# Attention for one query position: two K loads joined, and the last head's output split over two engines

## The chip, the cores and the metric

The kernel runs on one core of a Trainium2 chip. Times are device microseconds of one execution. Before the change, three runs gave 320.42, 319.57 and 319.09 us: a median of 319.57 us.

## The reference

```
q: (1, 16, 1, 256)   k, v: (1, 16, 8192, 256)   all bf16
scores = einsum("bhqd,bhkd->bhqk", q, k) * 256 ** -0.5
p      = softmax(scores)
out    = einsum("bhqk,bhkd->bhqd", p, v)      # (1, 16, 1, 256), bf16
```

There is one query row for each of 16 heads. Each head reads 8192 keys and 8192 values of 256 numbers once: 4.19 MB of K and 4.19 MB of V, so 134 MB in all.

## The kernel before

A head's K lies in a buffer of 128 partitions by 64 columns, where a column is one key's 256 numbers; partition p holds keys 64p to 64p + 63. There are two K buffers (`kbuf`, halves for even and odd heads) and two V buffers (`vbuf`). The DMA queue of SP carries every load in one written order (`ORDER`): `k0 k1 v0 k2 v1 k3 v2 ... k6 k7 v5 k8 ... k14 v12 k15 v13 v14 v15`. Most loads are whole heads (4096 KB). `CUTS` lists those that are cut into pieces at given columns, each piece a load of its own: k0 and k15 at column 34, and v13, v14 and v15. Every piece has a semaphore. For k0 and k15 the first piece shares the semaphore of all even or odd K loads (`k0`, `k1`), and the second has one named `kb`.

SP issues a load when its buffer is free. A K load of head h waits until VectorE (`kd`) and GpSimd (`tp`) have done with head h - 2 (L119, L120). A V load of head h waits for `pr`, which TensorE raises after the weighted sum of head h - 2 (L122).

The work of one head:

- Scores, columns 0 to 23: GpSimd multiplies four columns at once by the query (L182), and ScalarE sums each product along the row (L382). Two products may be under way (`sp`).
- Scores, columns 24 to 63: VectorE multiplies and sums one column in one instruction (L208), in four chunks of ten (loop over `c`). After the first chunk of head h it also takes the reciprocal of the softmax sum of head h - 2 (L195, `recips`) and the maximum of head h - 1 over the partitions (L199, `xmax`).
- The maximum: VectorE takes each partition's (L225), TensorE transposes that (L316), VectorE reduces it (L199), and TensorE spreads it to all partitions (L302).
- ScalarE takes the exponentials (L347, `expo`), in the middle of the next head's products.
- TensorE multiplies the exponentials by V (L265, `doubles`), two columns to a matmul, sums the exponentials (`total`, L252), and after ScalarE's drain of the sums (L358, `collect`, behind the last product of a head) gathers them into `ob` (L278). `ob` holds a head's 256 outputs as two halves, one in row 0 and one in row 32.
- ScalarE divides by the sum and writes row 0 and row 32 of `o_all` (L364, `final`), three heads behind.

TensorE goes through 18 rounds, one head's weighted sum two rounds after its scores. Each round waits for that round's maximum (`g`), then does the weighted sum, the total and the gather, and then waits for the next maximum (`m`).

Head 15 ends differently. The first 28 columns of its V go as above. The other 36 are multiplied straight into `ob` (L323), with a wait for each later piece of v15 (48 and 60). Then VectorE, and not ScalarE, divides (L231) rows 0 and 32 with those in between in one instruction. SP stores heads 0 to 14 (waiting for v15's last piece), then head 15 as two half rows of 256 B, and waits for both.

In the loop of VectorE the waits before each chunk are `k_waits` (the query's copy, and both K semaphores) and then, for the second piece of a cut load,

```
dve.wait_ge(sem("kb"), (h * 8 + c + 119) // 120 * 16 + 16)
```

which asks for k0's second piece from chunk 1 of head 0 on, and for k15's from chunk 1 of head 15 on. GpSimd has no such wait, since its columns all lie in the first piece.

Of the kernel before, what the change touches and what calls it, by code (L numbers as in the profile page):

```python
# [11 lines left out]
NPL = 24  # L12
GRP = 4
CH = 10
CUTS = {"k0": (0, 34), "k15": (0, 34), "v13": (0, 48), "v14": (0, 40), "v15": (0, 28, 48, 60)}
ORDER = "k0 k1 v0 k2 v1 k3 v2 k4 v3 k5 v4 k6 k7 v5 k8 v6 k9 v7 k10 v8 k11 v9 k12 v10 k13 v11 k14 v12 k15 v13 v14 v15"
LAST_PAIRED = 28
STRIP = 64
BLK = 32
ROWS = 97  # L20
AHEAD = {"k1": 16, "kb": 16, "sp": 2, "pr": 1, "cm": 2, "pv": 1, "fin": 3, "rc": 3, "ex": 1, "mT": 1, "g": 1, "nb": 1}
STREAM_AHEAD = ("v0", "v1", "v0_40", "v1_48")


def bass_standalone__mha_softmax__decode_kernel(nc: bass.Bass, q: bass.AP, k: bass.AP, v: bass.AP, out: bass.AP):
# [19 lines left out]
    def load(kind, h):  # L45
        cuts = CUTS.get(f"{kind}{h}", (0,)) + (J,)
        for n, (a, b) in enumerate(zip(cuts, cuts[1:])):
            name = "kb" if kind == "k" and n else f"{kind}{h % 2}" + (f"_{a}" if n else "")
            stream.append((kind, h, a, b, name))

    for name in ORDER.split():
# [2 lines left out]
    with contextlib.ExitStack() as ctx:  # L54

        def sb(name, shape, d):
            return ctx.enter_context(nc.sbuf_tensor(name, shape, d))
# [34 lines left out]
        identb = sb("identb", [P, P], BF16)  # L92
        ones_row = sb("ones_row", [1, P], FP32)
        ones_col = sb("ones_col", [P, 1], FP32)
        o_all = sb("o_all", [BLK + 1, H * HW], out.dtype)

        acc = ps("acc", [P, 2 * D])
        ob = ps("ob", [P, 512])
# [15 lines left out]
        @(lambda f: f(nc.sync))  # L114
        def _(sp):
            for kind, h, a, b, name in stream:
                if h >= 2 and a == 0:
                    if kind == "k":
                        sp.wait_ge(sem("kd"), (h - 1) * NC)  # L119
                        sp.wait_ge(sem("tp"), (h - 1) * NG)  # L120
                    else:
                        sp.wait_ge(sem("pr"), h + 2)  # L122
                buf = kbuf[:, h % 2 * J * D :] if kind == "k" else vbuf[h % 2]
                sp.dma_start(buf[:, a * D : b * D], src(k if kind == "k" else v, h)[:, a * D : b * D]).then_inc(  # L124
                    sem(name), 16
                )
            two = out.rearrange("b h s (two d) -> two (b h s) d", two=2)
            for a, b in ((0, LAST), (LAST, H)):
                if b < H:
                    sp.wait_ge(sem(stream[-1][-1]), 16)  # L130
                sp.wait_ge(sem("fin"), b + 3)
                rows = o_all[0 : BLK + 1 : BLK, a * HW : b * HW].rearrange("two (h d) -> two h d", d=HW)
                sp.dma_start(two[:, a:b, :], rows).then_inc(sem("o"), 16)
            sp.wait_ge(sem("o"), 32)
            sp.nop()

# [54 lines left out]
        @(lambda f: f(nc.vector))  # L191
        def _(dve):
            def recips(h, n, after=0):
                dve.wait_ge(sem("pr"), h - n + (3 + after))
                dve.reciprocal(recip[:, ds(back(h, n), 1)], tot[0 : BLK + 1, :]).then_inc(sem("rc"), 1)  # L195

            def xmax(h, n):
                dve.wait_ge(sem("mT"), h - n + 2)
                dve.tensor_reduce(g[:, :], mx[0:1, 0:P], AX.X, ALU.max).then_inc(sem("g"), 1)  # L199

            with dve.Fori(0, H) as h:
                par = dve.snap(h % 2)
                with dve.Fori(0, NC) as c:  # L203
                    k_waits(dve, h)
                    dve.wait_ge(sem("kb"), (h * 8 + c + 119) // 120 * 16 + 16)  # L205
                    for b in range(CH):
                        col = kbuf[:, ds(par * (J * D) + c * (CH * D) + (NPL + b) * D, D)]
                        ins = dve.scalar_tensor_tensor(  # L208
                            out=col,
                            in0=col,  # L210
                            scalar=SCALE,
                            in1=qrow[:, ds(par * 512, D)],
                            op0=ALU.mult,
                            op1=ALU.mult,
                            accum_out=S[:, ds(h * J + c * CH + (NPL + b), 1)],
                        )
                    ins.then_inc(sem("kd"), 1)
                    with dve.If(c == 0):
                        with dve.If(h > 1):
                            recips(h, 2)  # L220
                        with dve.If(h > 0):
                            xmax(h, 1)
                dve.wait_ge(sem("kd"), h * NC + NC)  # L223
                dve.wait_ge(sem("sp"), h * NG + (NG + 2))
                dve.tensor_reduce(m[:, :], S[:, ds(h * J, J)], AX.X, ALU.max).then_inc(sem("m"), 1)  # L225
            recips(LAST, 1)
            xmax(LAST, 0)
            recips(LAST, 0, 1)
            dve.wait_ge(sem("rc"), H + 3)
            dve.wait_ge(sem("pv"), H + 4)  # L230
            dve.tensor_scalar(  # L231
                out=o_all[:, LAST * HW : H * HW],
                in0=ob[0 : BLK + 1, 0:HW],
                scalar1=recip[:, LAST:H],
                scalar2=None,
                op0=ALU.mult,
            ).then_inc(sem("fin"), 1)
# [95 lines left out]
        @(lambda f: f(nc.scalar))  # L333
        def _(act):
            def q_copy(h):
                act.wait_ge(sem("qp"), h + 1)
                par = 0 if isinstance(h, int) else act.snap(h % 2)
                act.activation(out=q_now[:, ds(par * D, D)], in_=qrow[:, ds(par * 512, D)], func=ACT.Copy).then_inc(  # L338
                    sem("qb"), 1
                )  # L340

            def expo(h, n):
                act.wait_ge(sem("bc"), h - n + 2)
                act.activation(out=negb[:, :], in_=sm, func=ACT.Copy, scale=-1.0).then_inc(sem("nb"), 1)  # L344
                act.wait_ge(sem("nb"), h - n + 2)
                i = back(h, n)
                act.activation(  # L347
                    out=E[:, ds(i % 2 * EW, J)].rearrange("p (two x) -> p x two", two=2),
                    in_=S[:, ds(i * J, J)].rearrange("p (x two) -> p x two", two=2),
                    func=ACT.Exp,  # L350
                    bias=negb[:, :],
                    scale=1.0,
                    accum_out=lsum[:, :],
                ).then_inc(sem("ex"), 1)

            def collect(h, n):
                act.wait_ge(sem("pr"), h - n + 4)
                act.activation(out=comb[:, :], in_=acc[0:ROWS, :], func=ACT.Copy).then_inc(sem("cm"), 1)  # L358

            def final(h, n):  # L360
                act.wait_ge(sem("rc"), h - n + 4)
                act.wait_ge(sem("pv"), h - n + 4)
                i = back(h, n)
                act.activation(  # L364
                    out=o_all[:, ds(i * HW, HW)],
                    in_=ob[0 : BLK + 1, 0:HW],
                    func=ACT.Copy,
                    scale=recip[:, ds(i, 1)],
                ).then_inc(sem("fin"), 1)

            act.dma_start(q_sb[:, :], q[0, :, 0, :]).then_inc(sem("ldq"), 16)
            act.preload_act_table(ACT.Exp)
            q_copy(0)
            with act.Fori(0, H + 2) as h:
                with act.If(h < H):
                    q_copy(h + 1)
                with act.Fori(0, NG) as i:
                    with act.If(h < H):
                        act.wait_ge(sem("tp"), h * NG + i + 1)
                        for b in range(GRP):  # L380
                            part = prod[:, ds(i % 2 * (GRP * D) + b * D, D)]
                            ins = act.activation(  # L382
                                out=part,
                                in_=part,
                                func=ACT.Copy,
                                scale=SCALE,
                                accum_out=S[:, ds(back(h, 0) * J + i * GRP + b, 1)],
                            )
                        ins.then_inc(sem("sp"), 1)
                    with act.If(i == 1):  # L390
                        with act.If(h > 0):
                            with act.If(h < H + 1):
                                expo(h, 1)
                        with act.If(h > 2):
                            final(h, 3)
                with act.If(h > 1):
                    collect(h, 2)
            act.nop()


# [26 lines left out]
```

## Time and profile before

| | before |
|---|---|
| median of three runs | 319.57 us |
| the profiled execution | 318.72 us |
| its span in the profile | 317.1 us |
| granted TensorE clock, mean | 0.726 |
| VectorE busy | 232.5 us (73%) |
| GpSimd busy | 204.3 us (64%) |
| ScalarE busy | 190.6 us (60%) |
| TensorE matmuls busy | 123.5 us (39%) |
| read from memory | 134.23 MB, 423 GB/s over the span |
| load queue's packets | 98.7% of the 16 DMA engines' span |

In the profile PE is TensorE, DVE is VectorE, ACT is ScalarE, POOL is GpSimd and SP is SyncE; a q behind the name (DVEq, SPq) is that engine's instruction queue, where waits, register work and the issue of transfers happen. L208 is line 208 of the kernel. A row of the timeline gives a start, a length, the engine and the line, output and input, and in square brackets how long the engine had stood idle and what ended that. A row of groups gives the count, the busy time and the mean in ns. A row of the chain of waits gives start, length and what it was spent on; a load's length there runs from its issue to its landing.

### The profile page before, as it was taken

To read this page: it belongs to the slowest core of one execution; us is meant where nothing else is said; L and a number is where in the kernel's file an instruction comes from. 1 tells how busy PE (TensorE), PEld (TensorE's weight loads), DVE (VectorE), ACT (ScalarE), POOL (GpSimd) and SP (SyncE) were. 2 spreads that over 40 slices of the span, in tenths; PEclk is the share of its full clock that TensorE was granted. 3 is DMA by queue.
4 is the path that set the end of the run, shared out by engine and by line. 5 is a ranking of instruction groups with operands and counts; after the bars stand their busy time and mean duration, and the time that the engine had idled before them with its cause. 6 is when DMAs were issued, how large, how long until landed. Compare 5 with 4: busy or idle time off the path is not lost.

```text
span 317.1 us, 7815 instructions
## 1 busy us (share of the span) xinstructions
PE 123.5 (39%) x832; PEld 60.9 (19%) x832; DVE 232.5 (73%) x1329; ACT 190.6 (60%) x865; POOL 204.3 (64%) x115
## 2 busy tenths in 40 slices
PE   3001116262372723527182521706227061361855
PEld 1000003031130301213030310302113030121423
DVE  0797979497694967969797969679395893969700
ACT  2476737477373864777666757647386473868510
POOL 3788758395683857869686848578384874886400
PEclk9999999657565685757665585765957567585799
DMA  7999999999999999999999999999999999999995
GB/s 303 429 459 409 451 434 426 442 418 451 409 463 397 463 397 463 401 459 401 459 417 442 426 434 442 417 455 405 463 397 463 397 463 401 436 434 409 434 424 243
DMA packets 5685, 134.25 MB, mean 423 GB/s; under 512 B 676, under 2 KB 692, under 8 KB 948
## 3 DMA queue, kind: packets, MB, share of 16 engines
q1 hardware_dynamic: 5652, 134.23, 98.7%
q10 hardware_dynamic: 32, 0.01, 0.0%
q8 instruction: 1, 0.02, 0.0%
HBM read 134.23 MB, written 0.01 MB: 423 GB/s over the span
## 4 chain that ended last, share of the span: by engine, by line
DMA 56%; DVE 21%; issue 10%; DVEq 9%; PE 2%; SPq 1%
DMA kbuf<-in_k_dram 42%; DVE kbuf L208 20%; DMA vbuf<-in_v_dram 14%; DVEq L208 6%; PE acc L265 2%; DVEq L205 1%; DVEq L203 1%; DVEq L140 1%; SPq L124 1%; DVEq L139 0%; PE ob L323 0%; DVE g L199 0%; DVE recip L195 0%; DVEq L223 0%; DVEq L195 0%
## 5 line engine op out<-in xcount | busy, mean ns | idle before, releaser
L208 DVE SCALAR_TENSOR_TENSOR kbuf<-kbuf,qrow x640 | 223.8, 417 | 53.8 <-issue 27.8
L182 POOL TENSOR_TENSOR prod<-kbuf,q_now 128x1024 f32 x96 | 201.8, 2123 | 89.8 <-DMA kbuf<-in_k_dram 60.8
L382 ACT ACTIVATE prod<-prod x384 | 154.5, 403 | 74.9 <-POOL prod L182 68.6
L265 PE MATMUL acc<-vbuf,E 128*64 128x512 bf16 x494 | 85.5, 521 | 31.8 <-DMA vbuf<-in_v_dram 31.2
L382 ACT ACTIVATION_READ_ACCUMULATOR prod<-prod x384 | 71.7, 187 | 0.0
L208 DVE DVE_READ_ACCUMULATOR kbuf<-kbuf,qrow x640 | 52.8, 83 | 0.0
L265 PEld LDWEIGHTS acc<-vbuf,E 128*64 128x64 bf16 x494 | 36.2, 148 | 74.7 <-issue 34.4
L302 PE MATMUL mx<-g,ones_row 1*128 1x1 f32 x34 | 9.7, 351 | 75.5 <-DVE g L199 75.5
L278 PE MATMUL ob<-comb,sel 97*1 97x128 f32 x144 | 14.4, 335 | 52.0 <-ACT comb L358 52.0
L338 ACT ACTIVATE q_now<-qrow (+1 forms) x17 | 6.5, 383 | 28.7 <-PE qrow L242 28.6
L302 PEld LDWEIGHTS mx<-g,ones_row 1*128 1x128 f32 x34 | 8.2, 298 | 79.9 <-DVE g L199 79.5
L316 PE MATMUL mx<-ident,m 128*1 128x128 f32 x32 | 8.3, 352 | 25.9 <-DVE m L225 25.9
L278 PEld LDWEIGHTS ob<-comb,sel 97*1 97x1 f32 x144 | 5.6, 91 | 55.0 <-ACT comb L358 53.3
L225 DVE TENSOR_REDUCE m<-S 128x1 f32 x16 | 3.5, 220 | 13.8 <-ACT prod L382 12.5
L358 ACT ACTIVATE comb<-acc 97x512 f32<-97x512 f32 x16 | 9.2, 576 | 6.7 <-PE tot L252 6.7
L347 ACT ACTIVATE E<-S,negb x16 | 9.3, 583 | 4.1 <-ACT negb L344 4.1
L195 DVE RECIPROCAL recip<-tot 33x1 f32 (+1 forms) x16 | 2.5, 155 | 10.6 <-PE tot L252 10.6
L316 PEld LDWEIGHTS mx<-ident,m 128*1 128x1 f32 x32 | 3.1, 103 | 28.3 <-DVE m L225 26.9
L242 PE MATMUL qrow<-q_sb,identb 16*128 16x256 bf16 x18 | 6.0, 347 | 4.6 <-DMA q_sb<-in_q_dram 4.6
L364 ACT ACTIVATE o_all<-ob,recip 33x128 f32 x15 | 5.4, 362 | 1.4 <-PE ob L278 1.4
L347 ACT ACTIVATION_READ_ACCUMULATOR E<-S,negb 128x1 f32 x16 | 5.3, 330 | 0.0
L344 ACT ACTIVATE negb<-mx 128x1 f32<-128x1 f32 x16 | 2.5, 157 | 4.0 <-PE mx L302 4.0
(26 smaller groups left out, 23.3 us busy)
## 6 DMA issues: line engine op xcount, KB each, us to landing
kbuf<-in_k_dram SPq DMA_DIRECT2D x14, 4096.0 KB, 21.1
vbuf<-in_v_dram SPq DMA_DIRECT2D x13, 4096.0 KB, 27.1
kbuf<-in_k_dram SPq DMA_DIRECT2D x2, 2176.0 KB, 13.3
kbuf<-in_k_dram SPq DMA_DIRECT2D x2, 1920.0 KB, 17.5
vbuf<-in_v_dram SPq DMA_DIRECT2D x1, 3072.0 KB, 29.9
vbuf<-in_v_dram SPq DMA_DIRECT2D x1, 2560.0 KB, 19.7
vbuf<-in_v_dram SPq DMA_DIRECT2D x1, 1792.0 KB, 10.6
vbuf<-in_v_dram SPq DMA_DIRECT2D x1, 1536.0 KB, 23.0
```

What stands on the lines that cost most here:

```text
L182: pool.tensor_tensor(out=prod[:, b * GRP * D : (b + 1) * GRP * D].rearrange("p (b d) -> p b d", b=GRP), in0=kbuf[:, ds(par * (J * D) + i * ...
L208: ins = dve.scalar_tensor_tensor(out=col, in0=col, scalar=SCALE, in1=qrow[:, ds(par * 512, D)], op0=ALU.mult, op1=ALU.mult, accum_out=S[:, ...
L242: pe.matmul(qrow[:, ds(at * 512, D)], lhsT=identb[0:H, col].to_broadcast([H, P]), rhs=q_sb[:, :], start=True, stop=True,).then_inc(sem("qp ...
L265: ins = pe.matmul(acc[at : at + STRIP, :], lhsT=E[:, par * EW + j // 2 :][:, 0:STRIP], rhs=vbuf[par][:, j * D : (j + 2) * D], start=(j < 4 ...
L278: ins = pe.matmul(ob[row : row + 1, 0:HW], lhsT=sel[:, n : n + 1], rhs=comb[:, n * D + a : n * D + a + HW], start=(n == 0), stop=(n == 1), ...
L302: pe.matmul(sm, lhsT=ones_row[:, :], rhs=g[:, :], start=True, stop=True).then_inc(sem("bc"), 1)
L316: pe.matmul(mx[0:1, 0:P], lhsT=m[:, :], rhs=ident[:, :], start=True, stop=True).then_inc(sem("mT"), 1)
L338: act.activation(out=q_now[:, ds(par * D, D)], in_=qrow[:, ds(par * 512, D)], func=ACT.Copy).then_inc(sem("qb"), 1)
L347: act.activation(out=E[:, ds(i % 2 * EW, J)].rearrange("p (two x) -> p x two", two=2), in_=S[:, ds(i * J, J)].rearrange("p (x two) -> p x ...
L358: act.activation(out=comb[:, :], in_=acc[0:ROWS, :], func=ACT.Copy).then_inc(sem("cm"), 1)
L364: act.activation(out=o_all[:, ds(i * HW, HW)], in_=ob[0 : BLK + 1, 0:HW], func=ACT.Copy, scale=recip[:, ds(i, 1)],).then_inc(sem("fin"), 1)
L382: ins = act.activation(out=part, in_=part, func=ACT.Copy, scale=SCALE, accum_out=S[:, ds(back(h, 0) * J + i * GRP + b, 1)],)
```

## The change

- k0 and k15 leave `CUTS`: each is one load of 4096 KB with one semaphore. VectorE's wait on `kb` goes from its loop, and the semaphore with it.
- The last head's output: ScalarE, after its loop, divides row 0 of `ob` into the first 128 numbers of a new one-row tile `o_last`, and VectorE divides row 32 into the other 128. `o_all` keeps heads 0 to 14. The last store waits for both and writes `o_last`, one row of 512 B.
- Where a wait for the sums in `ob` (`pv`) stood behind the wait for the reciprocal (`rc`), it now stands ahead of it: in VectorE's last operation and in ScalarE's `final`.

```
-CUTS = {"k0": (0, 34), "k15": (0, 34), "v13": (0, 48), "v14": (0, 40), "v15": (0, 28, 48, 60)}
+CUTS = {"v13": (0, 48), "v14": (0, 40), "v15": (0, 28, 48, 60)}
...
-            name = "kb" if kind == "k" and n else f"{kind}{h % 2}" + (f"_{a}" if n else "")
+            name = f"{kind}{h % 2}" + (f"_{a}" if n else "")
...
-        o_all = sb("o_all", [BLK + 1, H * HW], out.dtype)
+        o_all = sb("o_all", [BLK + 1, LAST * HW], out.dtype)
+        o_last = sb("o_last", [1, D], out.dtype)
...
-            two = out.rearrange("b h s (two d) -> two (b h s) d", two=2)
-            for a, b in ((0, LAST), (LAST, H)):
-                if b < H:
-                    sp.wait_ge(sem(stream[-1][-1]), 16)
-                sp.wait_ge(sem("fin"), b + 3)
-                rows = o_all[0 : BLK + 1 : BLK, a * HW : b * HW].rearrange("two (h d) -> two h d", d=HW)
-                sp.dma_start(two[:, a:b, :], rows).then_inc(sem("o"), 16)
+            sp.wait_ge(sem(stream[-1][-1]), 16)
+            sp.wait_ge(sem("fin"), LAST + 3)
+            sp.dma_start(
+                out.rearrange("b h s (two d) -> two (b h s) d", two=2)[:, 0:LAST, :],
+                o_all[0 : BLK + 1 : BLK, :].rearrange("two (h d) -> two h d", d=HW),
+            ).then_inc(sem("o"), 16)
+            sp.wait_ge(sem("fin"), H + 4)
+            sp.dma_start(out[0, LAST, :, :], o_last[:, :]).then_inc(sem("o"), 16)
...
-                    dve.wait_ge(sem("kb"), (h * 8 + c + 119) // 120 * 16 + 16)
...
+            dve.wait_ge(sem("pv"), H + 4)
             dve.wait_ge(sem("rc"), H + 3)
-            dve.wait_ge(sem("pv"), H + 4)
+            row, a = halves[1]
             dve.tensor_scalar(
-                out=o_all[:, LAST * HW : H * HW],
-                in0=ob[0 : BLK + 1, 0:HW],
-                scalar1=recip[:, LAST:H],
+                out=o_last[:, a : a + HW],
+                in0=ob[row : row + 1, 0:HW],
+                scalar1=recip[0:1, LAST:H],
...
             def final(h, n):
+                act.wait_ge(sem("pv"), h - n + 4)
                 act.wait_ge(sem("rc"), h - n + 4)
-                act.wait_ge(sem("pv"), h - n + 4)
...
+            act.wait_ge(sem("pv"), H + 4)
+            act.wait_ge(sem("rc"), H + 3)
+            act.activation(out=o_last[:, 0:HW], in_=ob[0:1, 0:HW], func=ACT.Copy, scale=recip[0:1, LAST:H]).then_inc(
+                sem("fin"), 1
+            )
```

More of the change, by code (lines that the diff above doesn't have):

```diff
@@ L20 @@
 ROWS = 97
-AHEAD = {"k1": 16, "kb": 16, "sp": 2, "pr": 1, "cm": 2, "pv": 1, "fin": 3, "rc": 3, "ex": 1, "mT": 1, "g": 1, "nb": 1}
+AHEAD = {"k1": 16, "sp": 2, "pr": 1, "cm": 2, "pv": 1, "fin": 3, "rc": 3, "ex": 1, "mT": 1, "g": 1, "nb": 1}
 STREAM_AHEAD = ("v0", "v1", "v0_40", "v1_48")
```

## The prediction

> **What bounds the kernel now.** I read the page first for the share of each engine and of the DMA, then stretches of the span for the DMA's rate, then the chain of work that ended last, then the waits near both ends, where the change acts.
>
> From the page, the DMA row of the 40 slices and the queue that carries the loads:
>
> ```profile
> DMA  7999999999999999999999999999999999999995
> ...
> q1 hardware_dynamic: 5652, 134.23, 98.7%
> ```
>
> No compute engine is busy over 73% of the span, but the 16 DMA engines are at 9 tenths or more in every slice but the first and the last. The same in numbers, by stage: the middle, where only whole loads run; the stretch that holds the cut k15; the last stretch, with the cut V loads (columns: stretch, its length, five busy times, granted clock, DMA share, GB/s).
>
> ```profile
> core 0: us, PE busy (x) PEld busy (x) DVE busy (x) ACT busy (x) POOL busy (x), PEclk, DMA share, GB/s
> 42.20:246.20 204.00, 85.78 (x518) 41.60 (x517) 159.43 (x913) 129.77 (x594) 138.72 (x66) 0.66 1.00 432
> 246.20:292.40 46.20, 15.07 (x96) 7.69 (x96) 37.03 (x213) 30.02 (x139) 33.71 (x17) 0.65 1.00 428
> 292.40:314.00 21.60, 15.34 (x155) 7.95 (x157) 7.01 (x40) 7.37 (x30) 4.11 (x2) 0.89 1.00 421
> ```
>
> The share is 1.00 throughout, so the time is bytes over rate: 134.23 MB at 432 GB/s is 310.7 us of the span's 317.1. The bytes do not change. What the change can move is the start, the end, the few per cent between 421 and 432 GB/s, and any gap that it opens in the queue. A whole 4.19 MB load takes 4.19/0.432 = 9.7 us.
>
> The end of the chain of work that ended last (start, length, what):
>
> ```profile
> 299.20 14.74 DMA vbuf<-in_v_dram
> 313.94 0.04 issue
> 313.99 1.08 PE ob L323 x32
> 315.07 0.03 issue
> 315.09 0.02 DVEq L230
> 315.11 0.05 issue
> 315.17 0.34 DVE o_all L231
> ```
>
> The third piece of v15 lands at 313.94; from there it is 1.08 us of matmuls, 0.10 us until VectorE starts, 0.34 us of its one operation, and then the last store: 317.1 - 315.51 = 1.59 us.
>
> **Part 1: k0 in one piece.** Head 0's scores now wait for the whole of k0. Rows: VectorE's first column and the first of its second chunk, which waited for the second piece; from the chain, k0's and k2's loads; and the load of k8, for comparison.
>
> ```profile
> 9.50 0.42 DVE L208 SCALAR_TENSOR_TENSOR kbuf<-kbuf,qrow  x1 [9.50 <-issue]
> ...
> 13.68 0.42 DVE L208 SCALAR_TENSOR_TENSOR kbuf<-kbuf,qrow  x1 [0.68 <-DMA kbuf<-in_k_dram]
> ```
>
> ```profile
> 1.19 11.87 DMA kbuf<-in_k_dram
> ...
> 24.40 17.79 DMA kbuf<-in_k_dram
> ...
> 135.51 13.03 DMA kbuf<-in_k_dram
> ```
>
> The second piece landed at 1.19 + 11.87 = 13.06 and VectorE ran on 0.62 us later. With one piece the first chunk starts at about 13.7 in place of 9.50. VectorE had three chunks left at 13.68 and ended them at 24.40, 3.6 us each; now it has four, and ends at about 28.0. It is k2's load that waits for this (its buffer holds k0), so k2 is issued 3.6 us later. Cover: k2 was issued at 24.40 and landed at 42.19, so with 9.7 us of its own the load ahead of it, v0, ended at about 32.5. The issue stood 8.1 us ahead of that; it will stand 4.5 us ahead. Is that enough? k8 was issued at 135.51 and landed at 148.54, so only 3.3 us before its forerunner ended at about 138.8, and the engines stayed full there:
>
> ```profile
> 136.00:140.00 4.00, 1.76 (x11) 0.71 (x11) 1.76 (x10) 1.75 (x8) 3.14 (x2) 0.50 1.14 492
> ```
>
> (A share over 1 is a packet counted where it ended.) So I cost the delay at nothing. The next load that it could hurt is v2, which waits for head 0's weighted sum, which waits for the first chunk of head 2:
>
> ```profile
> 53.04 0.33 SPq L124 DMA_DIRECT2D vbuf<-in_v_dram  x1
> ```
>
> Its forerunner k3 ends at about 42.19 + 2 x 9.7 = 61.6, 8.6 us later; a delay of 3.6 us leaves 5.0. By head 3 it is gone, since a load pair takes 19.4 us and VectorE's head some 16.5 (below). If this cover failed, each microsecond past it would cost one.
>
> **Part 2: k15 in one piece.** GpSimd's head-15 rows, VectorE's first head-15 column and head 14's and 15's maximum, ScalarE's drain after head 15 (L358, issued behind its last product):
>
> ```profile
> 266.34 4.20 POOL L182 TENSOR_TENSOR prod<-kbuf,q_now 128x1024 f32 x2 [5.60 <-DMA kbuf<-in_k_dram]
> ...
> 281.12 4.20 POOL L182 TENSOR_TENSOR prod<-kbuf,q_now 128x1024 f32 x2 [0.82 <-DMA kbuf<-in_k_dram]
> ```
>
> ```profile
> 282.42 0.22 DVE L225 TENSOR_REDUCE m<-S 128x1 f32 x1 [1.22 <-ACT prod L382]
> 284.17 0.42 DVE L208 SCALAR_TENSOR_TENSOR kbuf<-kbuf,qrow  x1 [1.53 <-issue]
> ...
> 298.98 0.22 DVE L225 TENSOR_REDUCE m<-S 128x1 f32 x1 [0.26 <-DVE kbuf L208]
> ```
>
> ```profile
> 298.39 0.57 ACT L358 ACTIVATE comb<-acc 97x512 f32<-97x512 f32 x1
> ```
>
> GpSimd started head 15 at 281.12, as the first piece landed. The second, 30 of 64 columns or 1.97 MB, needs 4.6 us more at 428 GB/s: k15 is whole at 285.7. VectorE's head took 298.98 - 284.17 = 14.8 us, with its gap of 1.5 to 2 some 16.5; it starts at about 286.4 and ends near 301, so GpSimd with ScalarE decides. Head 14 shows that pair from a start set by the DMA: 266.34 to 282.42 is 16.1 us. So head 15's maximum comes at 285.7 + 16.1 = 301.8, 2.8 us later, and ScalarE's drain about 3.1 later. Bounds: GpSimd's whole 4.6, and the 2.2 by which VectorE's start moves. Take 3.1. Behind the drain stand TensorE's gather of head 13, the maximum's transpose, head 14's weighted sum, and head 15's. What TensorE waits for between 301 and the end:
>
> ```profile
> PE acc L265 <- DMA vbuf<-in_v_dram: 3.2, 3, 1.5
> PE ob L278 <- ACT comb L358: 1.5, 2, 0.8
> PE ob L323 <- DMA vbuf<-in_v_dram: 0.6, 1, 0.6
> ```
>
> In one chain it waits 3.2 + 0.6 = 3.8 us for loads that keep their times. A delay of 3.1 is eaten up there, with 0.7 to spare. Cost 0; at the upper bound 4.6 - 3.8 = +0.8 us.
>
> **Part 3: two cuts fewer.** SP issues two loads less (0.33 us each in the rows above, hidden by a queue that is full). Does a cut cost DMA time? The last stretch runs at 421 for 432 GB/s: 2.5% of 21.6 = 0.55 us over five extra pieces, 0.11 each. So two cuts give -0.2 us. Bounds: 0, and -2.1 if k0's whole start-up excess (13.06 less the 9.7 of a load, less 1.7 for the issue and the first bytes: the first slice's digit 7 leaves 1.6 to 2.4 of its 7.9 us idle) were the cut's, 1.7, and the 0.43 us (4/432 of 46.2) of the stretch with k15 too.
>
> **Part 4: the wait on "kb" leaves VectorE's loop.** Its register work:
>
> ```profile
> L205 DVEq FUSED_REGOPS  x64: 218/218/222, 8.6 to 294.4; - x64
> ```
>
> 64 x 0.218 = 14 us of VectorE's queue, much of it beside running columns. No load waits for VectorE with an empty queue, so it is worth 0 on the path (it trims the delays of parts 1 and 2 by up to 0.2 a chunk, which I leave out).
>
> **Part 5: the last head's output.** Before, one VectorE operation on 33 partitions; now ScalarE scales row 0 and VectorE row 32 into one row. ScalarE's last work before, its form of the operation, and both output stores:
>
> ```profile
> 310.88 0.60 ACT L358 ACTIVATE comb<-acc 97x512 f32<-97x512 f32 x1 [2.29 <-PE tot L252]
> ```
>
> ```profile
> L364 ACT ACTIVATE o_all<-ob,recip 33x128 f32 x15 | 5.4, 362 | 1.4 <-PE ob L278 1.4
> ```
>
> ```profile
> L133 SPq DMA_DIRECT2D out_dram<-o_all x2: 526/598/670, 314.6 to 315.5; - x2
> ```
>
> Columns per partition stay 128, so each operation keeps its time: 0.34 on VectorE, 0.36 on ScalarE, side by side: +0.02. The swapped order of the two waits: in the chain above the separate wait instruction is the later-written one, L230, and the operation starts 0.08 after it. With the reciprocal's wait written last, that one passes early: -0.05 to -0.08. ScalarE's last drain ends at 311.48, 3.6 us before the last matmul does, so its new instruction waits ready. Side by side or one after the other is shown by no row; if the two reads of one PSUM bank took turns, +0.36.
>
> [...]
>
> The last store carries 512 B as one row in place of two half rows. No row shows that shape: 0, with bounds of -0.2 (issue at the 0.33 of a wide load for 0.53) and +0.15 (the 0.67 of the longer store).
>
> **Sum.** 0 + 0 - 0.2 + 0 - 0.05 + 0 = -0.25 us on the profiled execution's 318.72, which itself stands 0.85 below the median of 319.57. On the median: 319.3.
>
> **Rivals.** (a) The end overruns: part 2's delay reaches TensorE at its full 4.6 us, in place of 3.1. For it: ScalarE stops for the exponentials in mid-head, so GpSimd may lose time again; the slack of 3.8 has only 0.7 left. Against: head 14's 16.1 us. It decides from 3.8 us on, and costs 0.8 at 4.6: 319.57 - 0.25 + 0.8 = 320.1, slower than before; beyond 5.6 it would pass 0.5%. (b) The queue runs dry at k2: for it, the 4.5 us left are near k8's 3.3, the least that I have seen to be harmless; against, k8's full window. It decides where k0 lands so late that k2's issue slips by more than 4.8, and a slip of 6 would cost about 1.2: 320.5. (c) Cuts are dear: -2.1 from part 3, so 317.4. For it, the slow first 11.9 us; against, the last stretch, where five cuts cost 0.55 together.
>
> [...]
>
> **Chances.** Hidden throughout, 319.3: 0.73. (a) 0.16, (b) 0.06, (c) 0.05. Under 0.5% (1.6 us, about what a measurement of this kernel can tell from no change) are the likeliest, (a) but for 0.03, and half of (b): same 0.89, slower 0.06, faster 0.05. The range takes in the run-to-run spread (0.5 below, 0.85 above the median) and (a): 318.4 to 320.6.
>
> **What would show it.** After: DMA share 1.00 across 28 to 36; VectorE's first column near 13.7; k2 issued near 28.0; the head-15 maximum near 301.8, TensorE's waits for v14 and v15 shrunk from 3.8 to about 0.7 in sum; the matmuls after v15's third piece starting within 0.1 of 313.9; ScalarE and VectorE starting together within 0.1 of the last matmul. Wrong if the DMA share dips behind v0, if TensorE no longer waits for v15, or if the last two operations do not overlap.

## The result, and the profile after

| | before | after |
|---|---|---|
| median of the runs | 318.93 us (7) | 321.12 us (7) |
| lowest to highest | 318.71 to 320.42 | 320.18 to 322.58 |
| the profiled execution | 318.72 us | 321.43 us |
| its span | 317.1 us | 319.8 us |

The change made the kernel slower: ratio 1.0068, 95% interval 1.0044 to 1.0091. The forecast was 319.3, within half a per cent of before; the 319.57 from which it started is the median of the first three of the seven runs. Ratios leave out any run that lies over 1.5% above the fastest of its kernel, which is one run in all, at 323.89 us, in the experiment with k15 cut at column 54.

The span grew by 2.7 us, all of it at the end. TensorE's timeline after the change, from head 13's weighted sum on (start, length, line, operation, count, idle time before it and what ended that):

```profile
292.25 5.14 PE L267 MATMUL acc<-vbuf,E 128*64 128x512 bf16 x32 [2.32 <-DMA vbuf<-in_v_dram]
297.23 0.20 PE L254 MATMUL tot<-ones_col,lsum 128*33 128x1 f32 x2
301.98 0.90 PE L280 MATMUL ob<-comb,sel 97*1 97x128 f32 x8 [4.55 <-ACT comb L360]
...
304.18 5.99 PE L267 MATMUL acc<-vbuf,E 128*64 128x512 bf16 x32
310.00 0.20 PE L254 MATMUL tot<-ones_col,lsum 128*33 128x1 f32 x2
310.89 0.60 PE L280 MATMUL ob<-comb,sel 97*1 97x128 f32 x8 [0.69 <-ACT comb L360]
312.69 1.70 PE L267 MATMUL acc<-vbuf,E 128*64 128x512 bf16 x14 [1.20 <-issue]
314.22 0.20 PE L254 MATMUL tot<-ones_col,lsum 128*33 128x1 f32 x2
315.49 0.60 PE L280 MATMUL ob<-comb,sel 97*1 97x128 f32 x8 [1.07 <-ACT comb L360]
316.00 2.27 PE L325 MATMUL ob<-vbuf,E 128*1 128x128 bf16 x72
```

The same part of the timeline before the change:

```profile
292.44 5.85 PE L265 MATMUL acc<-vbuf,E 128*64 128x512 bf16 x32 [3.87 <-DMA vbuf<-in_v_dram]
...
299.02 0.60 PE L278 MATMUL ob<-comb,sel 97*1 97x128 f32 x8 [0.69 <-ACT comb L358]
...
301.03 2.35 PE L265 MATMUL acc<-vbuf,E 128*64 128x512 bf16 x20 [0.39 <-DMA vbuf<-in_v_dram]
304.72 1.49 PE L265 MATMUL acc<-vbuf,E 128*64 128x512 bf16 x12 [1.34 <-DMA vbuf<-in_v_dram]
306.04 0.20 PE L252 MATMUL tot<-ones_col,lsum 128*33 128x1 f32 x2
306.93 0.60 PE L278 MATMUL ob<-comb,sel 97*1 97x128 f32 x8 [0.69 <-ACT comb L358]
309.00 1.70 PE L265 MATMUL acc<-vbuf,E 128*64 128x512 bf16 x14 [1.47 <-DMA vbuf<-in_v_dram]
...
312.09 1.28 PE L323 MATMUL ob<-vbuf,E 128*1 128x128 bf16 x40
313.99 1.06 PE L323 MATMUL ob<-vbuf,E 128*1 128x128 bf16 x32 [0.62 <-DMA vbuf<-in_v_dram]
```

Before, TensorE waited four times for V between 300 and 314. After, it waits there for none: the data lie there, and TensorE is late. Three things are to be read from it. ScalarE's drain let the gather start at 301.98, 3 us later than the 299.02 of before. Head 14's sum then took 5.99 us where it had taken 2.35 + 1.49 = 3.84. And the last matmul ended at 318.27 in place of 315.05, 3.2 later.

The reason for the 5.99 stands in the granted clock, in stretches of the span (columns as in the prediction), first before, then after:

```profile
302.00:304.00 2.00, 1.38 (x14) 0.49 (x10) 0.00 (x0) 0.00 (x0) 0.00 (x0) 1.00 1.02 432
```

```profile
298.00:302.00 4.00, 0.02 (x2) 0.02 (x4) 1.89 (x12) 3.56 (x17) 1.47 (x1) 1.00 0.96 410
302.00:304.00 2.00, 1.95 (x13) 0.98 (x13) 0.28 (x1) 0.00 (x0) 0.00 (x0) 0.53 0.99 419
```

Before, the clock was full (1.00) from 298 to the last matmul. After, TensorE stood idle from 297.4 to 302.0 (0.02 us busy of 4 in the first row of after), and the clock, still full in that row, was at half as it took up work again (0.53 from 302 to 304), and stayed there to 308 (0.50).

At the very end the change gained time. The last operations and the store after the change:

```profile
318.31 0.36 ACT L402 ACTIVATE o_last<-ob,recip 1x128 bf16<-1x128 f32 x1 [2.87 <-PE ob L325]
318.31 0.34 DVE L233 TENSOR_SCALAR o_last<-ob,recip 1x128 bf16<-1x128 f32 x1 [3.69 <-PE ob L325]
318.69 0.29 SPq L135 DMA_DIRECT2D out_dram<-o_last  x1
```

Both engines start 0.04 us after the last matmul, and run side by side on one PSUM tile, `ob`, in rows 0 and 32: both from 318.31 on, 0.36 and 0.34 us, as long as ScalarE's and VectorE's operations on 33 of its partitions took before (0.36 and 0.34). From the last matmul's end to the span's it is 319.8 - 318.27 = 1.53 us, where it was 317.1 - 315.05 = 2.05: a gain of 0.52. So 3.2 lost and 0.5 gained make the 2.7.

### The profile page after: what moved, and what is told of

It reads as the page before. It is cut to its first block, busy times and chain, and to the rows that moved or that the text cites. A ratio compares the mean times of both kernels' runs of the same rounds, so it can differ in the third digit from the quotient of the medians.

```text
span 319.8 us, 7750 instructions
## 1 busy us (share of the span) xinstructions
PE 127.6 (40%) x832; PEld 62.6 (20%) x832; DVE 228.3 (71%) x1329; ACT 190.9 (60%) x866; POOL 204.2 (64%) x115
## 4 chain that ended last, share of the span: by engine, by line
DMA 40%; issue 14%; DVE 13%; POOL 9%; ACT 7%; DVEq 6%; PE 5%; ACTq 4%; POOLq 2%
DMA kbuf<-in_k_dram 40%; DVE kbuf L209 12%; POOL prod L184 9%; ACT prod L384 6%; DVEq L209 4%; PE acc L267 2%; ACTq L384 1%; PE ob L280 1%; POOLq L184 1%; DVEq L141 1%; ACT comb L360 1%; PE ob L325 1%; DVEq L205 1%; ACTq L379 1%; DVE g L201 0%
## 5 line engine op out<-in xcount | busy, mean ns | idle before, releaser
L209 DVE SCALAR_TENSOR_TENSOR kbuf<-kbuf,qrow x640 | 220.9, 407 | 50.0 <-DMA kbuf<-in_k_dram 33.9
L267 PE MATMUL acc<-vbuf,E 128*64 128x512 bf16 x494 | 88.6, 537 | 30.6 <-DMA vbuf<-in_v_dram 28.8
L267 PEld LDWEIGHTS acc<-vbuf,E 128*64 128x64 bf16 x494 | 37.4, 152 | 75.5 <-issue 39.6
L209 DVE DVE_READ_ACCUMULATOR kbuf<-kbuf,qrow x640 | 47.4, 74 | 0.0
L201 DVE TENSOR_REDUCE g<-mx 1x1 f32<-1x128 f32 x16 | 4.2, 261 | 1.4 <-PE mx L318 1.4
```

The lines of the kernel that those rows point to most:

```text
L209: ins = dve.scalar_tensor_tensor(out=col, in0=col, scalar=SCALE, in1=qrow[:, ds(par * 512, D)], op0=ALU.mult, op1=ALU.mult, accum_out=S[:, ...
L267: ins = pe.matmul(acc[at : at + STRIP, :], lhsT=E[:, par * EW + j // 2 :][:, 0:STRIP], rhs=vbuf[par][:, j * D : (j + 2) * D], start=(j < 4 ...
```

## The experiments

Executions of one kernel scatter here by some 2.6 us (33 runs of the kernel before in one comparison lay between 318.44 and 321.02), so a ratio is read with its interval. Each ratio is against the kernel before on the same chip.

**One part at a time.** First the change with k15 cut again:

```
-CUTS = {"v13": (0, 48), "v14": (0, 40), "v15": (0, 28, 48, 60)}
+CUTS = {"k15": (0, 34), "v13": (0, 48), "v14": (0, 40), "v15": (0, 28, 48, 60)}
...
+                    dve.wait_ge(sem("kb"), (h * 8 + c + 119) // 120 * 16 + 16)
```

> The changed kernel with k15 cut at column 34 again (k0 whole, output split kept). Theory A, the whole loss comes from k15: TensorE's rounds at the end start 3 us later, and what was meant to eat that up was not there. Then this is faster than before by the two gains that the profile of the changed kernel shows, 0.46 us at the last store and about 0.1 us at the loads: 318.93 - 0.6 = 318.4, ratio 0.998. Theory B, k0's late start or the loop without the wait also costs: then between 319 and 321.

Measured: 319.78 us, ratio 1.0012 (0.9988 to 1.0037). Of the 2.2 us lost, 1.3 are back, but the 318.4 of theory A is missed. The lowest runs (318.06 and 318.28) are near it; half of the twelve lie between 319.4 and 319.9. In the profiled one the loads were late: v15's third piece let TensorE go on at 315.51, for 313.99 before.

k15 alone in one piece:

```
-CUTS = {"k0": (0, 34), "k15": (0, 34), ...
+CUTS = {"k0": (0, 34), ...
...
-                    dve.wait_ge(sem("kb"), (h * 8 + c + 119) // 120 * 16 + 16)
+                    dve.wait_ge(sem("kb"), (h * 8 + c + 239) // 240 * 16 + 16)
```

(The wait on `kb` stays in VectorE's loop, for k0's second piece alone.)

> The kernel before with k15 alone in one piece (k0 cut, one VectorE operation at the end). Theory A: TensorE's head-14 sum starts near 304 and takes 6 us, and the span grows by 3.2: about 322.0, ratio 1.010, slower than the changed kernel's 321.12. Theory B: less than that, 319.5 to 321, the rest being k0's.

Measured: 321.69 us, ratio 1.0082 (1.0050 to 1.0113). k15's single load is enough for the loss. TensorE shows the same picture: gather at 302.06 after 3.75 us of idling, head 14's sum from 304.38, 5.05 us long. The clock fell at about 300.4 here, earlier in the wait than after the change (302.1), and was full again earlier in the sum.

k0 alone in one piece:

```
-CUTS = {"k0": (0, 34), "k15": (0, 34), ...
+CUTS = {"k15": (0, 34), ...
```

(The wait on `kb` stays; its semaphore starts 16 higher, so that it passes at once for k0.)

> The kernel before with k0 alone in one piece (k15 cut, the wait on the second piece kept, one VectorE operation at the end). Theory A, k15 alone costs: 318.8, no difference. Theory B, k0 costs too, through the loads: v2 is issued near 58 in place of 53, the 16 DMA engines fall out of step between 60 and 66 us and their share there drops from 1.01 to 0.91 to 0.95 as in the run with k15 cut again; all later loads land 0.9 to 1.7 us later, and the time is 319.8 to 320.5, ratio 1.003 to 1.005.

Measured: median 320.02, before 318.72; ratio 1.0017 (0.9992 to 1.0041). The medians are 1.3 us apart, as theory B has it, but the interval reaches below 1. The run with k15 cut again and the one with the split alone (next) differ in k0's cut alone too, and their medians, 319.78 and 318.72, lie apart the same way. In the profiled execution GpSimd's wait for k3 ended at 62.88 in place of 62.24, and TensorE's for v7 at 179.57 in place of 178.22: the loads were late. But the fall of the DMA share between 60 and 66 us that theory B foretold is not in this trace (101.5%). Nor are the loads its whole loss: head 15's sum ran at half clock, 3.10 us for the 1.70 of before, though k15 was cut.

This run and the one with k15 cut again keep the wait on `kb` in VectorE's loop, and the changed kernel does not have it. SP's issues of k2 and k4, first after the change, then with k0 whole alone:

```profile
27.70 0.33 SPq L125 DMA_DIRECT2D kbuf<-in_k_dram  x1
...
60.32 0.33 SPq L125 DMA_DIRECT2D kbuf<-in_k_dram  x1
```

```profile
28.70 0.33 SPq L124 DMA_DIRECT2D kbuf<-in_k_dram  x1
...
62.01 0.33 SPq L124 DMA_DIRECT2D kbuf<-in_k_dram  x1
```

The profiles with k0 whole divide by that wait. The three with it (this one, k15 cut again, and k15 cut at 54 below) issue k2 at 28.70 to 28.75 and k4 at 62.01 to 62.08, and their loads are late: GpSimd's wait for k4 ends at 82.44 to 83.30, for 81.79 before. Of the four without it, three (the changed kernel, and below it with 14 matmuls added or with TensorE's last round written out) issue them at 27.70 to 27.91 and 60.32 to 60.50, and k4 is on time (81.63 to 81.82); the fourth, with 30 matmuls added, was late for a reason given below. So the experiments that take k0 by itself show a price that the changed kernel's trace does not have.

The output split alone, the changed kernel with both cuts and the wait for them put back:

```
-CUTS = {"v13": (0, 48), ...
+CUTS = {"k0": (0, 34), "k15": (0, 34), "v13": (0, 48), ...
...
+                    dve.wait_ge(sem("kb"), (h * 8 + c + 119) // 120 * 16 + 16)
```

> The kernel before with the output split and the one-row store alone. Theory A and B: the operation starts 0.05 sooner after the last matmul, the store's issue takes 0.29 for 0.53 and lands 0.2 sooner: 0.5 us less, 318.4, ratio 0.9985. Rival: the shorter store in the changed kernel came only from standing alone (the first store had been issued 4 us earlier); here the two follow within 1 us as before, and the gain is 0.1 or less.

Measured: 318.72 us, ratio 0.9979 (0.9957 to 1.0001); span 316.6 for 317.1. Its end in the timeline:

```profile
314.55 0.67 SPq L130 DMA_DIRECT2D out_dram<-o_all  x1
314.73 0.28 PE L326 MATMUL ob<-vbuf,E 128*1 128x128 bf16 x4
315.05 0.36 ACT L403 ACTIVATE o_last<-ob,recip 1x128 bf16<-1x128 f32 x1 [3.63 <-PE ob L326]
315.05 0.34 DVE L234 TENSOR_SCALAR o_last<-ob,recip 1x128 bf16<-1x128 f32 x1 [4.16 <-PE ob L326]
315.43 0.29 SPq L135 DMA_DIRECT2D out_dram<-o_last  x1
```

The two stores follow each other within 0.9 us, and the second still takes 0.29 to issue. So the shorter store comes from its shape and not from standing alone.

**The store's shape or the pair of engines.** VectorE does both halves into the row, ScalarE nothing:

```
+            for row, a in halves:
+                dve.tensor_scalar(out=o_last[:, a : a + HW], in0=ob[row : row + 1, 0:HW], ...
-            act.activation(out=o_last[:, 0:HW], in_=ob[0:1, 0:HW], ...
```

> The kernel before with the one-row store, but VectorE does both halves one after the other and ScalarE nothing. If the 0.5 us of the output split come from the store's shape (0.29 to issue for 0.53, landing 0.2 sooner) and the pair of engines only hides a second operation: the store starts 0.3 later than with the pair, span 316.9, lowest times near 318.4. If they come from the pair: as before, 318.7.

Measured: 318.48 us, ratio 0.9992 (0.9971 to 1.0014). The two operations took 0.71 us in sequence, from 315.26, and the store was issued at 316.00 in 0.29. Its span is 317.2, but its v15 pieces landed 0.2 later than in the run before. The store starts 0.74 after the operations begin, for 0.38 with the pair: the pair is worth 0.36 us against two operations in a row. Against the single operation of before (0.34 us on 33 partitions) it saves nothing; there the gain is the store's, and an operation that starts 0.04 us after the last matmul in place of 0.12. The medians cannot tell that apart.

**The clock.** In the changed kernel, 30 matmuls on a constant fill TensorE's wait for ScalarE's drain in round 15:

```
                 total(h)
+                with pe.If(h == LAST):
+                    for _ in range(30):
+                        pe.matmul(warm[0:STRIP, :]..., lhsT=identb[:, 0:STRIP], rhs=identb[:, :]..., start=True, stop=True)
                 pe.wait_ge(sem("cm"), h + 1)
```

> The changed kernel with 30 matmuls of 64 by 512 on a constant, into a tile that nobody reads, in TensorE's round of head 15, where it stood idle for 4.55 us waiting for ScalarE's drain. Theory A, with the clock as the larger half of the loss: the idle time falls to about 1 us, the granted clock stays at 1.00 from 296 on, the head-14 sum takes 3.8 us in place of 5.99, and the end comes 2.1 to 2.7 us earlier: 318.4 to 319.0. Theory C, the delay of 3 us alone does it and the clock follows its own course: no change, 321.

Measured: 323.25 us, ratio 1.0130 (1.0105 to 1.0155). It missed, because 30 of them took 6.64 us and not 3.6, and held the gather up to 306.43. The part it was built for did happen: the clock stayed at 1.00, and head 14's sum took 3.65 us. With 14 of them:

```
-                    for _ in range(30):
+                    for _ in range(14):
```

> The changed kernel with 14 such matmuls in place of 30 (those took 0.22 us each, not 0.12, and held up the gather by 4.4 us). They take 3.0 us of the 4.55 idle. Theory A: the clock stays at 1.00, the head-14 sum takes 3.65 us for 5.99, the gather is not held up, and the end comes 2.3 to 2.9 us earlier than in the changed kernel for the same loads; with the loads' own scatter 318.5 to 320.0. Theory C (the clock does not matter): 321.

Measured: 319.39 us, for the changed kernel's 321.12; ratio 1.0001 (0.9977 to 1.0025) against before. TensorE's rows:

```profile
297.71 3.19 PE L316 MATMUL warm<-identb 128*64 128x512 bf16 x14
301.99 0.60 PE L281 MATMUL ob<-comb,sel 97*1 97x128 f32 x8 [1.09 <-ACT comb L370]
...
303.68 3.65 PE L268 MATMUL acc<-vbuf,E 128*64 128x512 bf16 x32
...
309.98 3.20 PE L268 MATMUL acc<-vbuf,E 128*64 128x512 bf16 x14 [1.34 <-issue]
```

The gather starts at 301.99, where it started without them (301.98), so the wait was as long as before, and only the clock differs ahead of the sum. It takes 3.65 for 5.99. That useless work makes this kernel 1.7 us faster rules theory C out. The clock then fell one step later: head 15's sum took 3.20 for 1.70.

The same 14 matmuls, at the same place, in the kernel with k15 whole alone:

```
                 total(h)
+                with pe.If(h == LAST):
+                    fill(14)
```

> The kernel before with k15 whole (k0 cut, output not split: the run at 321.69) and 14 matmuls on a constant in TensorE's wait for ScalarE's drain in round 15. It takes the part of the clock out of k15's cost with k0 out of the way. Theory A (about 2.1 us of the loss is the halved clock in head 14's sum, the rest is 3 us of delay against 2.7 of true slack): the sum takes 3.65, and the median is 319.2 to 319.8, ratio 1.001 to 1.004. If the clock does not matter: 321.7. If an instruction fetch comes early (as at 6 us in the runs with 30 matmuls and with 12 fillers, where all loads landed 1.3 to 1.5 us later), 1.4 more.

Measured: 319.99 us, ratio 1.0034 (1.0012 to 1.0055), for 321.69 without the filling: again 1.7 us, though the two intervals overlap by a little. In the three profiles with k15 whole and the wait filled, head 14's sum took 3.65 us each time; in the three with the wait unfilled (the change, k15 alone, and the last round written out below) 5.05 to 5.99. In this run head 15's sum again ran at half clock (3.20 for 1.70), so the remaining 1.3 us do not show what the delay would cost at full clock throughout.

**How much delay is free.** The changed kernel with k15 cut at column 54, so that GpSimd's start was to move by about 3 us and not 4.4:

```
-CUTS = {"v13": (0, 48), ...
+CUTS = {"k15": (0, 54), "v13": (0, 48), ...
```

> The changed kernel with k15 cut at column 54. GpSimd starts head 15 near 284.0, in the middle between 281.1 (cut at 34) and 285.5 (whole); ScalarE's drain near 299.9, 1.5 us later than before. Theory A: TensorE's idle time before the gather is about 3 us and the slack left is about 2.7 us at full clock, so if the clock stays at 1.00 all is hidden: 318.4, as with the cut at 34. If the clock falls there too: up to 2.2 more on the head-14 sum, 319.5 to 320.5. Without any threshold (each microsecond of delay costs as much as the last) it is half of the loss: 319.8.

Measured: 320.54 us, ratio 1.0046 (1.0013 to 1.0078). Neither number of the forecast fits alone, since the runs fall into two groups: six from 318.47 to 319.84, six from 321.24 to 323.89. The profiled one is the longest. From it, GpSimd's start of head 15, and TensorE's rows:

```profile
286.81 4.20 POOL L184 TENSOR_TENSOR prod<-kbuf,q_now 128x1024 f32 x2 [3.85 <-DMA kbuf<-in_k_dram]
```

```profile
295.11 6.13 PE L268 MATMUL acc<-vbuf,E 128*64 128x512 bf16 x32 [3.63 <-DMA vbuf<-in_v_dram]
...
305.31 6.15 PE L268 MATMUL acc<-vbuf,E 128*64 128x512 bf16 x32
```

The half delay did not come about in this execution. Its loads were late (k4 at 83.30 for 81.79), GpSimd started head 15 at 286.81, later even than with k15 whole (285.51), and head 13's V came 2.7 us later than before. Its loss is that of late loads and of a half clock together (head 14's sum took 6.15), so how much delay is free stays open. That late loads, the clock or both divide the two groups is not shown, as no profile of a short run was taken.

**The end of TensorE's round.** The changed kernel with round 17 written out behind the loop:

```
-            with pe.Fori(0, H + 2) as h:
+            with pe.Fori(0, H + 1) as h:
...
+            doubles(1, 0, LAST_PAIRED, {0: (sem("v1"), H // 2 * 16 + 16)})
+            total(H + 1)
```

> The changed kernel with TensorE's round 17 written out behind its loop, so that it pays no loop end between the gather of head 14 and the sum of head 15, where it idled 1.20 us in the changed kernel with all data there. Theory A: that idle time falls to some 0.2 and the end comes 1.0 us earlier, 320.1. Rival: the 1.2 us is a wait for v15 or for the exponentials, and nothing changes.

Measured: 322.77 us, ratio 1.0084 (1.0053 to 1.0116): no gain. The 1.20 us of idle time is gone, head 15's sum starts at 311.46 right behind the gather, and the forecast of 1.0 us fell all the same. ScalarE's timeline tells why, first in this kernel, then in the changed one, then before:

```profile
312.22 0.36 ACT L371 ACTIVATE o_all<-ob,recip 33x128 f32 x1 [1.35 <-PE ob L280]
314.87 0.60 ACT L365 ACTIVATE comb<-acc 97x512 f32<-97x512 f32 x1 [2.29 <-issue]
```

```profile
312.19 0.36 ACT L366 ACTIVATE o_all<-ob,recip 33x128 f32 x1 [1.35 <-PE ob L280]
314.84 0.60 ACT L360 ACTIVATE comb<-acc 97x512 f32<-97x512 f32 x1 [2.29 <-PE tot L254]
```

```profile
308.23 0.36 ACT L364 ACTIVATE o_all<-ob,recip 33x128 f32 x1 [1.35 <-PE ob L278]
310.88 0.60 ACT L358 ACTIVATE comb<-acc 97x512 f32<-97x512 f32 x1 [2.29 <-PE tot L252]
```

In all three ScalarE's drain comes 2.29 us after its `final` ends, whether TensorE's total was ready at 310.74, 314.42 or already at 313.19. Between the two it goes through the empty rest of its loop over product groups. So from a gather's end to the next drain, 3.35 us (307.53 to 310.88, 311.49 to 314.84), ScalarE sets the pace, as long as TensorE's total is ready by then. In the unrolled kernel TensorE just waited 2.33 us for the drain, the clock was at half behind that wait (0.50 from 316 to 318), and its last 72 matmuls took 3.46 us for 2.27.

**Whether a late v2 explains k0.** The kernel before, with v2 held back:

```
                         sp.wait_ge(sem("pr"), h + 2)
+                        if h == 2:
+                            sp.wait_ge(sem("kd"), 3 * NC)
```

> The kernel before, with k0 cut as before, and v2's load held until VectorE has done with head 2 (one more wait on SP): v2 and k4 are issued together near 57.8, v2 4.8 us later than before. With k0 whole alone the median was 320.0 for 318.7, and the loads landed 0.6 us late from k3 on and 1.35 late at the end. If it is the late issue of v2, with a queue less deep at 58 to 62, that costs: the loads lag here too, and the median is 319.5 to 320.3. If it is k0's single piece itself or the later start: 318.7, as before.

Measured: 319.47 us, before on that chip 319.12; ratio 1.0009 (0.9987 to 1.0032). It cannot be told from before by its time. The trace shows a small lag: k4 0.35 us late (GpSimd's wait ends at 82.14 for 81.79), v7 0.7. The rows below are the busy tenths of the 16 DMA engines between 60 and 66 us in 40 slices: before, here, and with k15 cut again (k0 whole).

```profile
DMA  0000599900005999000059990000599900005999
```

```profile
DMA  0000999500009999900559999005099990050999
```

```profile
DMA  0005099960005999599055599990095599950955
```

Before, the packets come in bursts, every 1.2 us. With v2 late the bursts drift apart, and with k15 cut again more so (q1's share there fell to 91.4%); with k0 whole alone, whose loads were late too, they do not (101.5%). Nor does v2's issue sort the runs: the changed kernel issued it at 57.16 with its loads on time, k0 whole alone at 56.83 with its loads late. So a late v2 goes with a small lag, and does not explain k0's cost by itself. In this run, too, head 15's sum ran at half clock (3.17 for 1.70), with k15 cut.

**A version without the scatter.** With the output split alone, 12 matmuls in TensorE's short waits of the last three rounds:

```
                 total(h)
+                with pe.If(h >= LAST):
+                    fill(3)
...
                 gather().then_inc(sem("pv"), 1)
+                with pe.If(h == H):
+                    fill(3)
```

> The kernel before with the output split, and 12 matmuls on a constant in TensorE's short waits of the last rounds (3 after each total of rounds 15, 16 and 17, 3 after the gather of round 16; each 0.22 us, so 0.66 us in waits of 0.69, 0.69, 0.78 and 1.48). If the executions at 320.5 (9 of 33 before, and those at 320.0 with the output split) come from a clock that falls at the end, they go, and the median is 318.1 to 318.3, ratio 0.996. If they come from the loads, they stay: 318.7, ratio 0.998. If the fillers hold up the chain: up to 0.5 more.

Measured: 320.37 us, ratio 1.0037 (1.0024 to 1.0051). The scatter went (320.06 to 320.75, 12 runs), and the clock stayed at 1.00 from 300 to the end, but every run was at the late end. The load queue's view between 6 and 12 us has a row that the same stretch lacks without the fillers:

```profile
q8 instruction: 1, 0.02, 1.0%
```

One instruction fetch of 0.02 MB, which came at 313 in the kernel before, came at 10 us. GpSimd's wait for k2 ended at 44.16, for 42.90 with the output split alone, and every load after it was 1.2 to 2.3 us late. The kernel with 30 matmuls had its fetch in this stretch too, and its wait for k0 ended at 15.21 in place of the changed kernel's 13.63. So part of that run's loss was not TensorE's. With five fillers, at the second place alone:

```
+                with pe.If(h == H):
+                    fill(5)
```

> The kernel before with the output split and 5 matmuls on a constant after the gather of round 16, where TensorE idles 1.48 us, of which 1.2 us are the end of its round. If the run with 12 fillers lost only through the early instruction fetch at 6 us: with the fetch at 312 again, the median is 318.1 to 318.4 and the executions near 320 are rare, ratio 0.996 to 0.998. With the fetch early again: 320.0. If the fillers themselves hold up head 15's sum: 318.5 to 319.

Measured: 319.84 us, ratio 1.0031 (1.0015 to 1.0046). The fetch came at 310, into the last V loads: v15's later pieces let TensorE start at 313.26 and 315.16 for 312.05 and 313.95. The clock fell to 0.50 behind the first wait, and the last 32 matmuls took 1.87 for 1.06. So neither filled version pays, and the output split with both cuts kept has the best ratio that was measured: well ahead of the changed kernel (0.9979 for 1.0068), and ahead of the kernel before by 0.2%, with an interval that just reaches 1, so that it is not clearly told from it.

## Why the prediction was wrong

**Part 2, k15, is the step that failed:** its slack of 3.8 us, and the work behind the delay, which it took to keep its length. The delay itself was right: GpSimd started on the whole k15 at 285.51 (285.7 foretold), the maximum came at 301.60 (301.8), and ScalarE's drain at 301.35, 2.96 later (3.1). What it was set against, and what followed from it, were not.

- *The slack was 2.4 us, not 3.8.* I added up TensorE's waits for loads "in one chain". The 1.47 ahead of head 15's sum was no slack: beside it ran ScalarE's 3.35 us from the gather to its next drain, which came no earlier for an earlier sum (the last round written out showed that). That leaves 0.39 + 1.34, and 0.69 at the last matmuls (312.09 to 315.05 for an unbroken 2.27).
- *The delay did not stay 2.96.* I priced TensorE's work at its lengths of before, which were lengths at full clock (granted 1.00 from 298 on). Behind the idle time that the delay makes the clock was at half (0.53, then 0.50, from 302 to 308): the gather, transpose and spread on the way to head 14's sum took 0.58 us longer (it could have started at 301.03 - 0.39 = 300.64, and started at 304.18), and the sum itself 2.15.

So 2.96 + 0.58 + 2.15 = 5.7 us stood against 2.4: 3.3 over, where 3.2 were measured. By the same sum it would have been 2.96 - 2.4 = 0.5 over at full clock, and with the gain of 0.5 at the end the forecast would have held; no run had the full clock throughout and the loads on time to test that. That the sum's 2.15 hang on the clock was shown by filling the idle time; that the rest of the sum adds up so is worked out from the traces.

The warning stood in rows that I had quoted, a granted clock of 0.66 in the middle and 0.89 at the end, and in two that I had not: before the change, 32 matmuls took 5.85 us (292.44, with a granted clock of 0.50 to 296 and 0.76 from 296 to 298) and 20 took 2.35 (301.03, at 1.00). The runs do not fit one length of idling behind which the clock falls: it fell behind 4.55 us in the changed kernel (1.00 to 302, 0.50 from 302.25), about 2.1 us into the wait with k15 whole alone (work ended at 298.31), and behind a wait of 1.48 us with k0 whole alone (0.63 from 310 to 312, 0.52 from 312 to 314), and it stayed full across 1.47 us before (1.00 from 306 to 310). So the length of one wait does not settle it, and what does is not shown here.

**Rival (a)** named the right place, an overrun at the end, for a reason that did not come: the delay reached ScalarE's drain at 2.96 us and not at its full 4.6. Its price of 0.8 us had no clock in it, and its turning point was 3.8 for 2.4. That the time came out on its side is luck.

**Part 1, k0:** the steps came as foretold (k2 issued at 27.70, v2 at 57.16, all loads on time in the changed kernel's trace; k3 landed 0.17 us earlier than before). So the cover held in the changed kernel. Two pairs of medians agree: the changed kernel has 321.12 where k15 whole alone has 321.69, and with 14 matmuls added 319.39 for 319.99, 0.6 less both times, about what the output split gains by itself. In the three profiles that keep the wait on `kb`, k2 was issued 0.8 to 1.0 us later still, and the loads were late; that the later issue is what makes them late is not shown, as no run changed that alone.

**Part 3, the cuts:** -0.2 foretold; in the changed trace head 13's V let TensorE start at 292.25 for 292.44, -0.19. The same loads in the kernel with the last round written out gave 292.41, so the agreement is no evidence. **Part 4**, put at 0, was not tried alone. Yet with k0 whole, VectorE released k2's buffer 1.0 us later with the wait on `kb` in its loop than without it (28.70 for 27.70), so the term that was left out, 0.2 a chunk, used cover that part 1 needed. **Part 5:** no run before the result showed the +0.02 for two engines side by side, in place of +0.36 one after the other: it was my choice, and the change's trace shows it to be right (both from 318.31 on, 0.36 and 0.34 us). The wait's order was right too (0.04 us from the last matmul to the operation, for 0.12). The store was priced at 0 with a bound of -0.2, and gave about -0.45, since both its issue (0.29 for 0.53) and what follows it to the span's end (0.8 for 1.0) became shorter. **Rivals (b) and (c):** (b) did not happen in the changed kernel, whose loads were on time; (c) did not happen.

## What to carry to other kernels

An idle time in the row of an engine is slack only if no other engine's path of the same length runs beside it: follow the last wait through every engine that takes part before adding waits up. A delay that makes TensorE idle for some microseconds can cost twice, once as delay and once as half-speed work behind it (here 4.55 us of idling, and behind it 5.99 us for a sum that took 3.65 at a granted clock of 1.00), so lengths at full clock may not be carried over into a later start. An experiment that puts one part of a change back should be read with what it puts back beside it, here a wait in a loop. And a cut that seems idle in a kernel bound by its loads may be there for the last head alone.

## What the runs showed of the hardware

- A row of 512 B from one partition was stored with an issue of 0.29 us, two half rows of 256 B with 0.53, a wide load with 0.33.
- ScalarE and VectorE read rows 0 and 32 of one PSUM tile, `ob`, at the same time in 0.36 and 0.34 us (both from 318.31 on after the change, both from 315.05 on with the output split alone). Before, one operation on 33 partitions with the same 128 columns took as long: 0.36 us on ScalarE, 0.34 on VectorE.
- One instruction fetch of 0.02 MB among the loads went with a lag of 1.2 us and more in all later loads, in both runs that had it among the first loads (wait for k2 over at 44.16 for 42.90; for k0 at 15.21 for 13.63). Where it came differed by program, but not in order of length: at 313 us in the kernel before, at 310 with five matmuls more in the code, at 10 with six, between 306 and 312 with 14, between 6 and 12 with 30.
- Matmuls of 64 by 512 one behind the other took 0.22 us each (30 in 6.64), where those of the weighted sum, whose outputs go in turns to partitions 0 to 63 and 64 to 127, took 0.11 (32 in 3.65).
- The granted clock fell to 0.50 behind a wait of TensorE of 4.55 us (32 matmuls of the weighted sum then took 5.99 us, for 3.65 at 1.00) and behind one of 1.48 us (14 took 3.10, for 1.70), and stayed at 1.00 across one of 1.47 us.
